# Keys and queries loaded head by head, in transfers of 64 rows with two 2 KB pieces, and an earlier copy of the logits

## The chip, the core and the metric

The kernel runs on one core of a Trainium2 chip. The time of a run is the device time of that core in microseconds. The kernel before was timed three times: 556.40, 557.94 and 558.14 us, median 557.94 us. One more execution, the profiled one, took 561.26 us, and its trace spans 559.5 us from the first to the last instruction. All durations below come from that execution.

## The reference: what is computed

A sparse attention feeds a soft mixture of experts.

```python
# q, k, v: 8 batches x 8 heads x 576 positions x 64
scores = q @ k.T / 8
# heads 0..3: a query sees the 32 keys up to itself (local)
# heads 4..7: a query sees earlier keys at the same position modulo 32 (strided)
attn = softmax(where(mask, scores, -1e9));  x = attn @ v      # x: 4608 x 512

logits = x @ phi                                   # 32 slots, 4 for each of 8 experts
slot_input = softmax(logits, over tokens).T @ x    # 32 x 512
slot_out[e] = relu(slot_input[e] @ w1[e]) @ w2[e]  # w1: 512 x 1024, w2: 1024 x 512
out = softmax(logits, over slots) @ slot_out       # 4608 x 512
```

Everything is in float32. q, k and v hold 9.4 MB each, w1 and w2 16.8 MB each.

## The kernel before

One loop runs over the eight batches. A pass of it has two halves: L deals with the four local heads (x = 0), S with the four strided heads (x = 1). For each half the keys and queries come as rows of 2 KB: eight consecutive positions of one head are one row of 512 numbers, so a head is 72 rows. Eight of those rows (AR) go to the tile `rest`, the other 64 to the tiles `ld`. One `ld` tile holds four heads: partitions are 2 heads (j) times 64 rows, and the free dimension has two pairs of heads (a). `load_kq(b, x)` (lines 158 to 166) issues eight transfers for one half: for keys and for queries, and for each pair a, one of 256 KB into `ld` (line 165) and one of 32 KB into `rest` (line 166). All of them are issued by SP, in program order, together with the values (`load_v1`, line 171; `load_vs`, lines 177 to 181) and the expert weights (`load_weights`, lines 228 and 234, 512 KB each).

PE, ACT and DVE run in the order in which the code is written (a manual schedule); SP and POOL follow their own program order. Every instruction waits only for the data or the buffer that it needs.

`Tl(b)` and `Ts(b)` turn the rows over: `emit_T` makes 8 PE transposes (line 256) for queries, then 8 for keys, `emit_Tr` 8 small ones for `rest` (line 284), and ACT and DVE copy the results from PSUM to `ql`, `kbl`, `qal` (L half: lines 272, 275, 294, 295) and `qs`, `kbs`, `qas` (S half: lines 260, 264, 290, 298). The copies into one tile follow each other, so ACT and DVE alternate there. In the first L half of all, `Tl(0)` stands ahead of the loop; later `Tl(b + 1)` stands in pass b, after the transposes of the local probabilities (`emit_PT(b, 0)`, line 388) and the exponentials of the strided scores (`emit_exp(1)`, line 370).

A pass goes: local scores `emit_Sl` (`sl`), output transposes of the batch before (`emit_X`, `x`), the maximum, `emit_PT(b-1, 1)` and `emit_PTa` (`pt`, `pta`, lines 388 and 396, copied by ACT at 391 and 397), `Ts(b)`, the strided output of the batch before (`emit_AVs`, `as`; `emit_AVa`, `aa`), strided scores `emit_Ss` (`ss`), the slots' logits of the batch before (`emit_LG`, `lg`), their exponentials (`emit_soft`, line 491 on ACT), `emit_PT(b, 0)`, `emit_exp(1)`, `Tl(b+1)`, the copy of the logits from PSUM into `lall` (`st["keep"]`, defined in `emit_soft`, line 498, ACT), the transpose of the slots' exponentials (`emit_dT`, line 502 on PE, line 503 on DVE), the slot inputs (`emit_SI`, `si`) and the local output (`emit_AVl`, `al`). `emit_dT` writes into the same PSUM tile `lg` that the copy of line 498 reads, so it waits for that copy.

Loads are issued far ahead: the keys and queries of an L half right after the transposes of the L half before have read the `ld` tiles, those of an S half likewise. After the loop come the experts (`h`, `so`) and the output (`o`), which draw on 64 weight transfers.

Of the kernel before, what the change touches and what calls it, by code (L numbers as in the profile page):

```python
# [26 lines left out]
PN, TN = 72, 8  # L27
RW = 2 * PN
AUX = 64
AR = AUX // TN  # L30
# [37 lines left out]
def tile_sparse_attention_soft_moe(  # L68
# [12 lines left out]
    nc = tc.nc  # L81
# [28 lines left out]
    def pair2(nm):  # L110
        return psum.tile([P, 2, 512], F32, tag="pp", name=nm, bufs=3)
# [19 lines left out]
    ld = [[fix.tile([P, 2, 512], F32, tag=f"ld{x}{i}", name=f"ld{x}{i}") for i in range(2)] for x in range(2)]  # L131
    rest = fix.tile([P, 2, 512], F32, name="rest")
# [26 lines left out]
    def load_kq(b, x):  # L159
        h0 = 4 * x  # L160
        for i, src in enumerate((k, q)):
            r0 = 32 * x + 16 * i
            for a in range(2):
                rows = src[b, h0 + 2 * a:h0 + 2 * a + 2].rearrange("j (p n) d -> j p (n d)", n=TN)
                nc.sync.dma_start(out=ld[x][i][:, a], in_=rows[:, AR:PN])  # L165
                nc.sync.dma_start(out=rest[r0:r0 + 16, a], in_=rows[:, 0:AR])  # L166

    def load_v1(b):

        for a in range(2):  # L170
            nc.sync.dma_start(out=v1[64 * a:64 * a + 64, a],
                              in_=v[b, 2 * a:2 * a + 2].rearrange("j (s r) d -> r j s d", r=64))
# [63 lines left out]
    def weights_to(n):  # L236
        load_weights(n - len(wts))
# [3 lines left out]
    def two(t, n):  # L241
        return t[:, :, 0:n].rearrange("p a x -> p (a x)") if n == 512 else t[:, :, 0:n]
# [57 lines left out]
    def emit_Sl(b):  # L300
        ps = pair2(f"sl{b}")
        for j in range(2):
            mm(ps[:, j, :], idb, mask_l.unsqueeze(1).to_broadcast([P, 8, 64]), True, False)
        for j in range(2):
            for r in range(4):
                for c in range(4):
                    p0 = PN * j + AR + 4 * (4 * r + c)
                    mm(ps[32 * c:32 * c + 32, j, 128 * r:128 * r + 128], ql[:, j, 4 * r + c],
                       kbl[:, :, :, p0 - 4:p0 + 4].rearrange("p a n r -> p a r n"), False)
        u["sl"] = ps  # L310
# [48 lines left out]
    def emit_max(x):  # L359
        ps = u[("sl", "ss")[x]]  # L360
        _, mx = stats("mx", x)
        for s, m in zip(groups(ps, x), mx):
            nc.vector.tensor_reduce(out=m, in_=s, op=ALU.max, axis=AX.X)  # L363
        for s, o, m in zip(groups(ps, x), probs(x), mx):
            nc.vector.tensor_tensor(out=o, in0=s, in1=bc(m, s.shape[3]), op=ALU.subtract)
# [6 lines left out]
    def emit_sum(x):  # L372
        t, rz = stats("rz", x)
        for s, z in zip(probs(x), rz):
            nc.vector.tensor_reduce(out=z, in_=s, op=ALU.add, axis=AX.X)
        m = 20 if x else 16
        nc.vector.tensor_scalar_add(t[:, 0:m], t[:, 0:m], EPS)
        nc.vector.reciprocal(t[:, 0:m], t[:, 0:m])
        if x == 0:
            u["rz"] = rz[0]  # L380
            return
        for s, z in zip(probs(x), rz):
            nc.vector.tensor_tensor(out=s, in0=s, in1=bc(z, s.shape[3]), op=ALU.mult)

    def emit_PT(b, x, cp):
        ps = pair2(f"pt{b}{x}")
        for g in range(8):
            nc.tensor.transpose(out=ps[:, g // 4, 128 * (g % 4):128 * (g % 4) + 128],  # L388
                                in_=(pl[:, 2 * g:2 * g + 2].rearrange("p a k -> p (a k)") if x == 0 else
                                     psd[:, g].rearrange("p a k -> p (a k)")), identity=ident)  # L390
        cp(out=two(pt, 512), in_=two(ps, 512))  # L391

    def emit_PTa(b, cp):
        ps = small(f"pta{b}")
        for x in range(2):
            nc.tensor.transpose(out=ps[:, 128 * x:128 * x + 128], in_=psd[:, 8 + x].rearrange("p a k -> p (a k)"), identity=ident)
        cp(out=pta, in_=ps[:, 0:256])
# [16 lines left out]
    def emit_AVs(b, cps):  # L414

        ps = pair2(f"as{b}")
        for e in range(2):
            for w in range(2):
                for c in range(4):
                    for j in range(2):  # L420
                        for a in range(2):
                            d = slice(64 * a, 64 * a + NI)
                            o = 128 * (2 * e + w) + 32 * c
                            mm(ps[64 * j:64 * j + 64, a, o:o + 32], vs[d, j, 8 * w + 2 * c + e], pt[d, j, o:o + 32])
        for a in range(2):
            xv = xt[:, a, :].rearrange("p (c e h g) -> p c e h g", c=16, e=2, h=2)
            pv = ps[:, a].rearrange("p (e g c h) -> p c e h g", e=2, g=8, h=2)
            for e in range(2):
                cps[2 * a + e](out=xv[:, :, e], in_=pv[:, :, e])  # L429
# [19 lines left out]
    def emit_X(b, cp):  # L449
        ps = pair2(f"x{b}")  # L450
        for a in range(2):
            for r in range(4):
                nc.tensor.transpose(out=ps[:, a, 128 * r:128 * r + 128], in_=xn[:, r, 128 * a:128 * a + 128], identity=ident)  # L453
        cp(out=two(xt, 512), in_=two(ps, 512))  # L454
# [9 lines left out]
    st = {"m": None}  # L464

    def emit_LG(b, x):

        if x == 0:
            u["lg"] = psum.tile([P, 512], F32, tag="lg", name=f"lg{b}")
        for a in range(2):  # L470
            for t in range(4):
                mm(u["lg"][32 * t:32 * t + 32, 0:128], phs[:, 2 * x + a, :], xt[:, a, 128 * t:128 * t + 128],
                   x == 0 and a == 0, x == 1 and a == 1)
# [6 lines left out]
    def emit_soft(b, n, d):  # L480

        pv = u["lg"][:, 0:128 * n]
        bm = state.tile([P, 1], F32, tag="bm", name=f"bm{b}")
        nc.vector.tensor_reduce(out=bm, in_=pv, op=ALU.max, axis=AX.X)
        ngm = state.tile([P, 1], F32, tag="ngm", name=f"ngm{b}")
        if st["m"] is None:
            nc.vector.tensor_scalar_mul(ngm, bm, -1.0)
        else:
            nc.vector.scalar_tensor_tensor(out=ngm, in0=bm, scalar=-1.0, in1=st["m"], op0=ALU.mult, op1=ALU.min)
        zs = state.tile([P, 1], F32, tag="zs", name=f"zs{b}")  # L490
        nc.scalar.activation(out=d, in_=pv, func=AF.Exp, bias=ngm, accum_out=zs)
        al = None
        if st["m"] is not None:
            al = state.tile([P, 1], F32, tag="al", name=f"al{b}")
            nc.scalar.activation(out=al, in_=st["m"], func=AF.Exp, bias=ngm, scale=-1.0)
        st["m"], st["zs"] = ngm, zs
        u["d"], u["al"] = d, al
        st["keep"] = lambda: nc.scalar.copy(out=lall[:, b:b + n, :].rearrange("p v t -> p (v t)"), in_=pv)  # L498
# [25 lines left out]
    nc.scalar.activation(out=wac, in_=wac, func=AF.Exp)  # L524
    load_kq(0, 0)
    load_kq(0, 1)
    load_v1(0)
    load_vs(0)
# [11 lines left out]
    def Ts(b):  # L540
        emit_T(b, 1, 1, [ACT])
        emit_exp(0)
        emit_T(b, 1, 0, [ACT, DVE])
        emit_Tr(b, 1, [ACT, DVE, ACT, DVE, ACT])
# [3 lines left out]
    for b in range(B):  # L548

        emit_Sl(b)  # L550
        if b > 0:
            emit_X(b - 1, ACT)
        emit_max(0)
        if b > 0:
            emit_PT(b - 1, 1, ACT)
            emit_PTa(b - 1, ACT)
            load_v1(b)
        Ts(b)
        weights_to(2 * b + 2)
        if b < B - 1:  # L560
            load_kq(b + 1, 1)
        emit_sum(0)
        if b > 0:
            emit_LG(b - 1, 0)
            emit_AVs(b - 1, [DVE, ACT, DVE, ACT])
            emit_AVa(b - 1, [ACT, ACT, ACT])
            load_vs(b)
        if b == B - 1:
            weights_to(NWBUF + 5)

        make_v2()
        emit_Ss(b)
        emit_max(1)
        if b > 0:
            emit_LG(b - 1, 1)
            emit_XB(b - 1, ACT)
            emit_soft(b - 1, 1, dd[:, 0])
        emit_PT(b, 0, ACT)
        emit_exp(1)
        if b < B - 1:  # L580
            weights_to(3 * b + 3)
            Tl(b + 1)
        if b < B - 2:
            load_kq(b + 2, 0)
        elif b == B - 2:
            weights_to(NWBUF + 2)
        else:
            weights_to(NWBUF + 11)
        if b > 0:
            st["keep"]()  # L590
            emit_dT(b - 1, 1, u["lg"][:, 128:256], dd[:, 1])
            emit_SI(b - 1)
        emit_AVl(b)
        emit_sum(1)
    weights_to(NWBUF + 12)

    b = B - 1
# [321 lines left out]
```

## Time and profile before

| | before |
|---|---|
| median of 3 runs | 557.94 us |
| profiled execution | 561.26 us (span 559.5 us) |
| PE busy (matmuls) | 312.9 us, 56% of the span |
| DVE busy | 176.0 us, 31% |
| ACT busy | 136.4 us, 24% |
| POOL busy | 43.0 us, 8% |
| bytes moved | 73.31 MB, mean 131 GB/s |
| TensorE clock granted, mean | 0.696 of full speed |

How to read it: the shares are means over two quite different stretches. Up to some 447 us the loop over the batches runs, with 49 to 175 GB/s in the slices of the page; from there to the end the transfers move 213 to 382 GB/s. No engine is busy for more than 56% of the span, so what bounds the kernel is told by who waits for whom, not by the shares. A released wait is named by what came last; an idle time that stands in brackets in a row is the time the engine stood still just before that row.

### The profile page before, as it was taken

The page shows a single profiled execution, that of the slowest core. Times are in us where ns is not written, and L with a number is a line of the kernel's source. Part 1 is how long each engine was busy: PE and PEld are TensorE (multiplying, and loading weights), DVE is VectorE, ACT ScalarE, POOL GpSimd, SP SyncE. Part 2 cuts the span into 40 slices and gives each one's busy share as a digit, 9 for nine tenths or more (in the row PEclk, how much of TensorE's full clock was granted, in tenths as well). Part 3 has the DMA queues.
Part 4 walks back from the last instruction along what each step waited for, and adds up shares of the span by engine and source line. Part 5 has one row for each costly group of instructions (what it writes and reads, how often), then busy time and mean ns, then how long its engine had stood idle before and what let it go on. Part 6 is the DMA issues. An engine that isn't in the chain of part 4 may idle for free.

```text
span 559.5 us, 10346 instructions
## 1 busy us (share of the span) xinstructions
PE 312.9 (56%) x4477; PEld 226.7 (41%) x4477; DVE 176.0 (31%) x369; ACT 136.4 (24%) x297; POOL 43.0 (8%) x43
## 2 busy tenths in 40 slices
PE   3153328443856376636572657165705697779990
PEld 1043225332545245523461445044503474643660
DVE  1030306041522043305230424034402423336781
ACT  1022103232133114311330233021402132211471
POOL 5001100002000200011000200020002003001000
PEclk7565758695767567757675677558956856789996
DMA  2114131223141215121513142313321398699999
GB/s 56 51 52 111 58 116 52 84 71 95 59 150 52 80 64 174 56 80 52 175 67 81 51 136 105 85 49 101 139 84 49 91 292 298 213 310 325 382 368 325
DMA packets 66156, 73.31 MB, mean 131 GB/s; under 512 B 25664, under 2 KB 51648, under 8 KB 66112
## 3 DMA queue, kind: packets, MB, share of 16 engines
q1 hardware_dynamic: 65152, 72.36, 39.7%
q8 instruction: 35, 0.57, 0.4%
q10 hardware_dynamic: 960, 0.30, 0.3%
q14 instruction: 9, 0.07, 0.0%
HBM read 63.22 MB, written 9.44 MB: 130 GB/s over the span
## 4 chain that ended last, share of the span: by engine, by line
DMA 43%; PE 27%; SPq 23%; DVE 2%; issue 2%; ACT 1%; DVEq 0%
DMA ld<-in_q_dram 41%; SPq L166 20%; PE t L256 7%; PE as L246 3%; PE h L737 3%; PE so L835 3%; SPq L165 2%; PE tr L284 2%; PE o L863 2%; DMA ld<-in_k_dram 2%; PE lg L246 2%; PE ss L246 1%; PE si L246 1%; PE aa L246 1%; PE al L246 1%
## 5 line engine op out<-in xcount | busy, mean ns | idle before, releaser
L256 PE MATMUL t<-cf,ld 128*128 128x128 f32 x256 | 59.9, 413 | 182.0 <-DMA ld<-in_q_dram 180.8
L256 PEld LDWEIGHTS t<-cf,ld 128*128 128x128 f32 x256 | 48.4, 216 | 191.5 <-DMA ld<-in_q_dram 105.0
L275 DVE COPY ql<-t 64x512 f32<-64x512 f32 x8 | 5.5, 693 | 148.1 <-ACT ql L275 148.1
L187 POOL COPY v<-v 32x1024 f32<-32x1024 f32 x16 | 16.6, 1035 | 423.8 <-DMA v<-in_v_dram 423.3
L275 ACT COPY ql<-t 64x512 f32<-64x512 f32 x24 | 13.9, 580 | 133.0 <-PE t L256 126.8
L264 DVE COPY kbs<-t 64x1024 f32<-64x1024 f32 x8 | 9.8, 1228 | 90.5 <-ACT kbs L264 90.5
L246 PE MATMUL sl<-kbl,ql 128*32 128x128 f32 x512 | 29.7, 396 | 3.1 <-ACT kbl L294 3.1
L454 ACT COPY xt<-x 128x1024 f32<-128x1024 f32 x8 | 8.1, 1014 | 80.3 <-PE x L453 80.3
L246 PEld LDWEIGHTS al<-v,pt 128*32 128x32 f32 x512 | 22.8, 163 | 10.7 <-issue 9.2
L246 PE MATMUL al<-v,pt 128*32 128x128 f32 x512 | 25.8, 385 | 0.0
L260 ACT COPY qs<-t 128x1024 f32<-128x1024 f32 x8 | 8.1, 1012 | 68.3 <-PE t L256 68.3
L246 PEld LDWEIGHTS sl<-kbl,ql 128*32 128x32 f32 x512 | 18.4, 127 | 15.0 <-ACT kbl L294 4.8
L246 PE MATMUL as<-pt,vs 36*64 36x32 f32 x1024 | 23.1, 256 | 2.2 <-issue 2.2
L246 PEld LDWEIGHTS as<-pt,vs 36*64 36x64 f32 x1024 | 22.0, 178 | 4.8 <-issue 4.4
L502 PE MATMUL lg<-cf,dd 128*128 128x128 f32 x7 | 3.3, 475 | 29.0 <-ACT lall L498 29.0
L246 PE MATMUL ss<-kbs,qs 128*32 128x72 f32 x512 | 15.6, 291 | 3.9 <-issue 2.2
L391 ACT COPY pt<-pt 128x1024 f32<-128x1024 f32 x16 | 16.2, 1010 | 6.2 <-PE pt L388 6.2
L272 DVE COPY kbl<-t 64x512 f32<-64x512 f32 x16 | 11.1, 694 | 19.9 <-ACT kbl L272 19.9
L188 POOL COPY v<-v 32x1024 f32<-32x1024 f32 x16 | 16.6, 1035 | 0.9
L246 PE MATMUL lg<-xt,phs 128*32 128x128 f32 x288 | 15.4, 353 | 1.0 <-ACT xt L429 1.0
L363 DVE TENSOR_REDUCE mx<-ss 128x16 f32<-128x576 f32 (+1 forms) x16 | 8.7, 586 | 22.7 <-PE ss L246 22.7
L284 PEld LDWEIGHTS tr<-cf,rest 32*128 32x128 f32 x128 | 13.7, 199 | 5.3 <-issue 4.6
(192 smaller groups left out, 532.4 us busy)
## 6 DMA issues: line engine op xcount, KB each, us to landing
wb<-in_moe_w_dram SPq DMA_DIRECT2D x41, 512.0 KB
ld<-in_k_dram SPq DMA_DIRECT2D x32, 256.0 KB
ld<-in_q_dram SPq DMA_DIRECT2D x32, 256.0 KB
v<-in_v_dram SPq DMA_DIRECT2D x16, 288.0 KB
vs<-in_v_dram SPq DMA_DIRECT2D x16, 288.0 KB
ld<-in_moe_w_dram SPq DMA_DIRECT2D x4, 512.0 KB
v<-in_moe_w_dram SPq DMA_DIRECT2D x3, 512.0 KB
xt<-in_moe_w_dram SPq DMA_DIRECT2D x3, 512.0 KB
```

Source lines behind the costliest of these rows:

```text
L165: nc.sync.dma_start(out=ld[x][i][:, a], in_=rows[:, AR:PN])
L166: nc.sync.dma_start(out=rest[r0:r0 + 16, a], in_=rows[:, 0:AR])
L187: nc.gpsimd.tensor_copy(out=v2[r + 32:r + 64, a], in_=v1[r:r + 32, a, :, 1:9])
L188: nc.gpsimd.tensor_copy(out=v2[r:r + 32, a], in_=v1[r + 32:r + 64, a, :, 0:8])
L246: nc.tensor.matmul(out=out, lhsT=lhsT, rhs=rhs, start=start, stop=stop, skip_group_check=True)
L256: nc.tensor.transpose(out=tp[:, a, P * n:P * n + P], in_=src[:, a, P * n:P * n + P], identity=ident)
L275: cps[2 * a + e](out=ql[d, :, :, 16 * e:16 * e + 16].rearrange("p j t (r n) -> p (j t) r n", n=4), in_=tp[r, a].rearrange("p (n t r) -> p ...
L284: nc.tensor.transpose(out=tp[:, :, a, :, n, :], in_=rest[32 * x:32 * x + 32, a, P * n:P * n + P], identity=ident[32 * x:32 * x + 32, 32 * ...
L391: cp(out=two(pt, 512), in_=two(ps, 512))
L737: nc.tensor.matmul(out=ph[x][32 * e:32 * e + 32, :], lhsT=sit[:, c, 32 * (4 * g + e):32 * (4 * g + e) + 32], rhs=wts[16 * g + 4 * c + e][: ...
L835: nc.tensor.matmul(out=pos[x][32 * e:32 * e + 32, 0:256], lhsT=hts[g][:, c, 32 * e:32 * e + 32], rhs=wt[:, 256 * e:256 * e + 256], start=( ...
L863: nc.tensor.matmul(out=pq[:, 256 * y:256 * y + 256], lhsT=cts[vb][:, 128 * (2 * (t % 2) + t // 2):128 * (2 * (t % 2) + t // 2) + 128], rhs ...
```

## The change

Two edits. In `load_kq` each transfer now takes one head j of both pairs (64 rows, each with two pieces of 2 KB, one for each pair) in place of both heads of one pair (2 times 64 rows of one piece). The number of transfers, their bytes, their pieces of 2 KB and the places where the data lands are the same. In the loop, `st["keep"]()` moves from behind `Tl(b+1)` to right behind `emit_soft`.

```diff
         for i, src in enumerate((k, q)):
             r0 = 32 * x + 16 * i
-            for a in range(2):
-                rows = src[b, h0 + 2 * a:h0 + 2 * a + 2].rearrange("j (p n) d -> j p (n d)", n=TN)
-                nc.sync.dma_start(out=ld[x][i][:, a], in_=rows[:, AR:PN])
-                nc.sync.dma_start(out=rest[r0:r0 + 16, a], in_=rows[:, 0:AR])
+            rows = src[b, h0:h0 + 4].rearrange("(a j) (p n) d -> j p a (n d)", j=2, n=TN)
+            for j in range(2):
+                nc.sync.dma_start(out=ld[x][i][64 * j:64 * j + 64], in_=rows[j, AR:PN])
+                nc.sync.dma_start(out=rest[r0 + AR * j:r0 + AR * j + AR], in_=rows[j, 0:AR])
...
             emit_soft(b - 1, 1, dd[:, 0])
+            st["keep"]()
         emit_PT(b, 0, ACT)
         emit_exp(1)
...
         if b > 0:
-            st["keep"]()
             emit_dT(b - 1, 1, u["lg"][:, 128:256], dd[:, 1])
```

On SP, the queue that issues the loads, the piece at the end of the first batch's loads reads as follows in the kernel before (`ld_107` is the S half's query tile, `v_115`, `vs` and `val` hold values; behind each name stands the shape of what is written, rows first).

```order
L165 DMA ld_107<-in_q_dram 128x1x512
L166 DMA rest<-in_q_dram 16x1x512
L171 DMA v_115<-in_v_dram 64x18x64 x2
L177 DMA vs<-in_v_dram 36x2x1024
L179 DMA val<-in_v_dram 64x2x64
```

On the same queue, at the same place, the changed kernel has these.

```order
L165 DMA ld_107<-in_q_dram 64x2x512
L166 DMA rest<-in_q_dram 8x2x512
L171 DMA v_115<-in_v_dram 64x18x64 x2
L177 DMA vs<-in_v_dram 36x2x1024
L179 DMA val<-in_v_dram 64x2x64
```

Nothing moved in the queue; lines 165 and 166 have another shape. On the source side the list of pieces of line 165 was 2 heads of 64 rows each and is now 64 rows of 2 heads each; the transfers of the values already had 64 (or 36) rows as the first step of both lists.

On ACT, in the second pass (b = 1), behind the slots' exponentials (line 491), this is the difference (`lall` is the copy of the logits, `ql` and `kbl` are the copies of `Tl(2)`).

```order
 L491 ACTIVATE dd,zs_760<-lg_586,ngm_758 128x128
-L391 COPY pt<-pt_762 128x1024
-L370 ACTIVATE psd<-psd 128x16x36
-L370 ACTIVATE psd<-psd 128x256
-L275 COPY ql<-t_776 64x32x16 x3
-L272 COPY kbl<-t_789 64x4x2x64 x2
-L294 COPY kbl<-tr_802 64x2x4x8 x4
 L498 COPY lall<-lg_586 128x128
+L391 COPY pt<-pt_763 128x1024
+L370 ACTIVATE psd<-psd 128x16x36
+L370 ACTIVATE psd<-psd 128x256
+L275 COPY ql<-t_777 64x32x16 x3
+L272 COPY kbl<-t_790 64x4x2x64 x2
```

The copy of line 498 now stands ahead of the copy of the transposed probabilities, of the exponentials and of the copies that wait for the loads. The orders on PE, DVE and POOL are the same as before.

## Rows read from the trace of the kernel before

**Rows 1.** The page: shares of the chain that ended last, by engine and line.

```profile
DMA 43%; PE 27%; SPq 23%; DVE 2%; issue 2%; ACT 1%; DVEq 0%
DMA ld<-in_q_dram 41%; SPq L166 20%; PE t L256 7%; PE as L246 3%; PE h L737 3%; PE so L835 3%; SPq L165 2%; PE tr L284 2%; PE o L863 2%; DMA ld<-in_k_dram 2%; PE lg L246 2%; PE ss L246 1%; PE si L246 1%; PE aa L246 1%; PE al L246 1%
```

**Rows 2.** Waits, whole span: who waited for whom, us, times, longest.

```profile
PE t L256 <- DMA ld<-in_q_dram: 180.8, 28, 16.4
ACT ql L275 <- PE t L256: 126.8, 8, 25.4
ACT qs L260 <- PE t L256: 68.3, 8, 17.8
```

**Rows 3.** Windows: length, busy of PE to POOL, clock, DMA share, GB/s.

```profile
290.00:296.00 6.00, 0.00 (x0) 0.00 (x0) 0.14 (x1) 2.54 (x7) 0.00 (x0) 0.85 0.13 51
298.00:299.00 1.00, 0.00 (x0) 0.00 (x0) 0.00 (x0) 0.00 (x0) 0.00 (x0) 0.50 1.07 231
336.00:337.00 1.00, 1.00 (x59) 0.80 (x52) 0.52 (x1) 0.56 (x2) 0.00 (x0) 1.00 1.06 389
341.00:345.00 4.00, 4.00 (x96) 3.15 (x92) 0.83 (x2) 1.15 (x5) 0.00 (x0) 0.50 0.15 55
480.00:485.00 5.00, 4.50 (x173) 3.57 (x171) 0.42 (x1) 1.66 (x3) 0.00 (x0) 0.80 0.03 9
```

**Rows 4.** Timeline of SP: start, duration, transfer issued.

```profile
296.25 6.54 SPq L171 DMA_DIRECT2D v<-in_v_dram  x2
306.41 0.76 SPq L166 DMA_DIRECT2D rest<-in_k_dram  x1
312.00 4.99 SPq L166 DMA_DIRECT2D rest<-in_q_dram  x1
```

**Rows 5.** Timeline, an L half: start, duration, engine, instruction, [idle before it].

```profile
288.90 1.04 PE L388 MATMUL pt<-cf,pl 128*128 128x128 f32 x8
291.61 0.99 ACT L370 ACTIVATE psd<-psd 128x576 f32<-128x576 f32 x2
305.91 2.82 PE L256 MATMUL t<-cf,ld 128*128 128x128 f32 x12 [4.92 <-DMA ld<-in_q_dram]
307.06 0.58 ACT L275 COPY ql<-t 64x512 f32<-64x512 f32 x1 [14.46 <-PE t L256]
313.74 0.27 ACT L498 COPY lall<-lg 128x128 f32<-128x128 f32 x1
313.75 0.23 DVE L295 COPY qal<-tr 64x64 f32<-64x64 f32 x1 [0.27 <-ACT kbl L294]
314.06 0.47 PE L502 MATMUL lg<-cf,dd 128*128 128x128 f32 x1 [4.34 <-ACT lall L498]
314.57 0.29 DVE L503 COPY dd<-lg 128x128 f32<-128x128 f32 x1 [0.59 <-PE lg L502]
```

**Rows 6.** Timeline, the S half after it.

```profile
326.37 0.39 ACT L397 COPY pta<-pta 128x256 f32<-128x256 f32 x1
326.55 0.63 PE L256 MATMUL t<-cf,ld 128*128 128x128 f32 x4 [0.98 <-ACT pt L391]
333.59 1.01 ACT L260 COPY qs<-t 128x1024 f32<-128x1024 f32 x1 [6.82 <-PE t L256]
```

**Rows 7.** Timeline, the first batch.

```profile
28.57 0.58 ACT L275 COPY ql<-t 64x512 f32<-64x512 f32 x1 [25.45 <-PE t L256]
35.27 3.74 PE L246 MATMUL sl<-kbl,ql 128*32 128x128 f32 x64 [3.08 <-ACT kbl L294]
53.06 1.01 ACT L260 COPY qs<-t 128x1024 f32<-128x1024 f32 x1 [17.84 <-PE t L256]
```

**Rows 8.** Timeline of PE: two strided outputs, and a gap that no engine releases.

```profile
279.24 3.64 PE L246 MATMUL as<-pt,vs 36*64 36x32 f32 x128
336.38 2.06 PE L246 MATMUL as<-pt,vs 36*64 36x32 f32 x127
340.64 0.31 PE L246 MATMUL as<-pt,vs 36*64 36x32 f32 x1 [2.20 <-issue]
```

## The prediction

> **What bounds the kernel now.** I read the chain that ended last first. Transfers hold 43% of it and SP's issuing 23%, together 66% or 369 us, nearly all in the query loads and in line 166, which issues the `rest` transfers [rows 1]. Then the list of waits: PE stood 180.8 us for loads of `ld`, and behind PE stood ACT, 126.8 us before its first copy of an L half and 68.3 us before its first copy of an S half, 8 times each [rows 2]. So nearly every half ends in a wait for its keys and queries, although they are asked for a whole pass ahead.
>
> The windows tell why they are late. In 290 to 296 us only key and query loads run, and they hold 0.13 of the 16 DMA engines, which is two of the 16, at 51 GB/s; in 298 to 299 us, when a value transfer lands (SP issued it from 296.25 us on), the share is 1.07 at 231 GB/s; with weights it is 1.06 at 389 GB/s [rows 3, 4]. The value transfers begin with a list of 64 rows, the key and query loads with a list of two heads. SP then stands 4.99 us in line 166, and 256 KB at 51 GB/s are 5.1 us: it waits for room behind the transfers before [rows 4]. A half moves 1.18 MB, so 23 us of every half are taken by two engines.
>
> The Trainium skill's page "DMA: Bandwidth & Descriptors", section "Why a DMA increments its semaphore by 16 and not by 1", says that a transfer from SP is spread over the largest number of engines up to 16 that divides the slowest dimension on both sides. By it the old shape gets 2 and the new one 16 (8 for `rest`), and the 0.13 agrees with the 2.
>
> **The change part by part.** The sum is made against the profiled execution, 561.26 us (span 559.5, some 1.8 around it), which is 3.3 us above the median shown.
>
> *The loads.* Number, bytes and pieces stay; the first list becomes 64 rows, as in the value transfers. No row shows this very shape, so I bound its rate by 231 GB/s (the 64-row value transfer with 256 B pieces) and 389 GB/s (weights in 4 KB pieces) above, and 51 GB/s below, where nothing is won. I take 231, the row whose row count is the same. A pass then needs 2.36 MB of keys and queries and 1.18 MB of values at 231, 15.3 us, and three weights of 0.52 MB at 389, 4.0 us: 19 us. SP needs at most 16 issues at 0.76, the two value transfers at 6.54 and a dozen more at 0.76, some 28 us [rows 3, 4]. Both are below the 34 us that I find for a pass below, and each set is asked for about one pass ahead. So the wait goes whole, and what is late next decides the gain.
>
> *L halves, passes 1 to 7.* PE ends the local probabilities' transposes at 289.94. With the rows there, it goes on to 8 query transposes at 0.158 us (0.63 for 4), done by 291.2. ACT, though, has its exponentials until 292.60 and starts its copies then instead of at 307.06: its idle 14.46 goes whole, and ACT is late next, not PE [rows 5, 6]. Over the seven: 126.8 less the first batch's 25.4 is 101.4 us.
>
> *S halves, passes 1 to 7.* ACT is free at 326.76 and PE starts its transposes at 326.55 either way. Eight take 1.27, some 0.2 pass until ACT starts, so `qs` starts at about 328.0 instead of 333.59, and 1.2 of the idle 6.82 stay [rows 6]. Over the seven: 68.3 less 17.8 is 50.5, less 7 x 1.2: 42.1 us.
>
> *First batch.* SP's first eight issues and 1.18 MB at 231 GB/s (5.1 us) put the queries at about 8 us, 8 transposes at 0.235 (2.82 for 12) and the step to ACT make 10.1 for the first copy instead of 28.57: 18.5 us. In its S half PE is free when `sl` ends at 39.01; 8 transposes at 0.235 and 0.2 give 41.1 instead of 53.06: 12.0 us [rows 5, 7]. Ends: 3 us more or less on the first.
>
> The Trainium skill's page "SBUF — State Buffer", section "Door 1: The DMA port swizzle", says that bandwidth follows from how many of the 16 ports the partitions reach, and 64 partitions in a row reach half of them, half of some 436 GB/s. It speaks against halves of 64 rows; 231 is near that half. By it the sum keeps its value, since 231 is what I reckon with; at the weights' rate the first batch would gain 2 us more.
>
> *The copy of the logits.* It costs ACT 0.27 either way. Today PE's transpose at 314.06 waits for it, and DVE's copy follows at 314.57. Moved, the transpose runs during ACT's copies, and DVE's copy follows its own last `qal` copy, at 313.98: 0.6 won, less the 0.27 by which ACT's chain of copies now starts later, 0.3 a pass, 2 us in seven [rows 5]. Of PE's 4.34 us of idle before that transpose only this comes back, since the copies ahead of it must end anyway.
>
> *The clock.* TensorE is granted 0.50 (1.2 GHz) in stretches after PE stood for loads, as in 341 to 345, and 1.00 (2.4 GHz) in 336 to 337, where PE had been at work for some us; the strided output takes 3.64 us at the low level and 2.06 at the high one [rows 3, 8]. Without the loads' wait PE runs from the L half's scores through the S half almost without a pause. That is worth nothing at the least (ACT and DVE copies bind) and at most what an S half costs PE more at the low clock: 1.6 from this row and, I estimate, 1.1 from the strided scores and the transposes behind it, 2.7. Against it stands the 2.20 us gap that PE shows in 340.64 without any releaser [rows 8]; loads hide such gaps now. I take 1.5 a pass, 10.5 us.
>
> *Tail.* Behind the last S half nothing waits for keys or queries. Its weights are asked for by buffers that come free; with the share at 0.03 in 480 to 485 us they have room, so I cost it at nothing [rows 3]. If that cover is gone, some 5 us.
>
> Sum: 101.4 + 42.1 + 30.5 + 2 + 10.5 = 186.5, so 561.3 becomes 374.8; less the 3.3 by which the profiled execution stands above the median, 371.5, said as 371. A pass, now 56.1 us (333.59 less 53.06, over the five passes between [rows 6, 7]), loses 22.3 of it (the terms over seven) and goes to 34.
>
> **The rivals.**
> 1. *Other work comes in the loads' place for more than I allow*: the low clock stays, since PE still stands for the copies of each L half, as it did 4.34 us before line 502 [rows 5], and a gap like that of 2.20 us opens twice a pass. For it: the gap stands in a stretch of high clock, which there will be more of. Against: most passes show no gap like it. 371 + 10.5 + 14 x 2.2 = 412 at the worst, 385 to 412.
> 2. *More speed*: the clock is high throughout, also in the slot inputs and the local output, 1.5 us more a pass, and the S halves give their full 2.7: 371 - 10.5 - 8.4 = 352, 345 to 356. Against: in each L half PE still waits for the copies.
> 3. *The change doesn't do what it says*: the new shape too runs on two engines at 51 GB/s. The waits stay and the copy's 2 us are hidden behind them: 558. For it: the destination is still 128 rows in all and the pieces are as before. Against: the 1.07 of the 64-row transfers. The skill's page "DMA: Bandwidth & Descriptors" has a rule of the like outcome in "Rules for kernel authors": two transfers to disjoint halves of the partitions gain nothing, one of 128 is to be used. By that rule the time would stay at 558; the trace bears it out poorly, since the 128-row transfer here holds but 0.13.
> 4. *Slower*: the transfer of one head goes to one engine, as a transfer of two heads now goes to two. Then 51 GB/s become 25.5 and the 369 us of the chain double: 927. It decides below 51 GB/s. Against: the value transfers take two heads too and hold all engines.
>
> **How the numbers follow.** Chances: forecast 0.71 (its own range 357 to 385: the clock's term between 0 and 19, the start's 3, the tail's 5), rival 1 0.12, rival 2 0.11, rival 3 0.04, rival 4 0.02. The range of 8 in 10 leaves out the far ends of rivals 1 and 2 and all of 3 and 4: 350 to 397. A change under 0.3% can't be told from none here. Faster are the forecast, rivals 1 and 2: 0.94. Within 0.3% is rival 3, 0.04; slower rival 4, 0.02.
>
> **What would show it.** The DMA share near 1 while `ld` loads run, and line 166 at 0.8 us instead of 5; no row of PE waiting for `ld` except in the first batch; ACT's idle before L275 near nothing and before L260 near 1.2; TensorE at 1.00 in the strided output of most passes; the transpose of line 502 ahead of ACT's last copies; a pass of 33 to 36 us. Wrong it would be if line 166 still stood for us, if PE waited for values, or if the weights were late behind the last pass.

## The result, and the profile after

The changed kernel takes 354.18 us (median of 4, 350.55 to 358.08) against 557.17 us before in the same comparison: a ratio of 0.6306 [0.6272, 0.6341]. Two further comparisons gave 356.24 us, 0.6379 [0.6352, 0.6406], and 355.72 us, 0.6318 [0.6279, 0.6357]. The times are medians of all executions and the ratios those of the fast ones alone, since some executions of one and the same kernel run 1% or 2% longer at a lower granted clock. The forecast was 371 us; the time lies inside the range of 350 to 397 and 3 us below the likeliest case's own range, 357 to 385. The profiled execution took 350.55 us, which is the fastest of them; its span is 348.8 us and its mean granted clock 0.869, where before it was 0.696.

The page of the changed kernel: the chain by engine, and PE's group of strided outputs (busy us, mean ns).

```profile
PE 52%; ACT 21%; DVE 17%; issue 4%; DMA 3%; DVEq 0%; SPq 0%; ACTq 0%
L246 PE MATMUL as<-pt,vs 36*64 36x32 f32 x1024 | 16.5, 220 | 0.0
```

DMA and SP's issuing, two thirds of the chain before [rows 1], are 3% now. What is left is PE, ACT and DVE handing work to each other. The waits over the whole span, who for whom, us, times and longest:

```profile
PE si L246 <- DVE dd L503: 44.3, 7, 7.4
ACT ql L275 <- PE t L256: 9.3, 1, 9.3
ACT qs L260 <- PE t L256: 4.9, 1, 4.9
PE t L256 <- DMA ld<-in_q_dram: 4.7, 1, 4.7
```

Against [rows 2], PE's wait for loads went from 180.8 us to 4.7, and ACT's two waits behind PE from 126.8 and 68.3 us to 9.3 and 4.9; all that is left of the three stands in the first batch. At the head of PE's list stands another now: PE before the slot inputs (`si`), 44.3 us in seven. Most of it was there before, ahead of line 502: 29.0 us in seven, 4.34 of them in [rows 5]. The timeline of an L half shows it (start, duration, engine, instruction, idle before it and what ended that):

```profile
158.87 1.04 PE L388 MATMUL pt<-cf,pl 128*128 128x128 f32 x8
159.74 1.91 PE L256 MATMUL t<-cf,ld 128*128 128x128 f32 x16
161.57 1.01 ACT L370 ACTIVATE psd<-psd 128x576 f32<-128x576 f32 x2
162.19 0.33 PE L502 MATMUL lg<-cf,dd 128*128 128x128 f32 x1
162.46 0.58 ACT L275 COPY ql<-t 64x512 f32<-64x512 f32 x1
165.95 0.48 SPq L166 DMA_DIRECT2D rest<-in_q_dram  x1
169.14 0.23 DVE L295 COPY qal<-tr 64x64 f32<-64x64 f32 x1 [0.27 <-ACT kbl L294]
169.40 0.29 DVE L503 COPY dd<-lg 128x128 f32<-128x128 f32 x1
169.84 1.93 PE L246 MATMUL si<-xn,dd 128*32 128x512 f32 x8 [7.32 <-DVE dd L503]
171.52 3.67 PE L246 MATMUL al<-v,pt 128*32 128x128 f32 x64
```

Beside [rows 5], the 16 transposes follow the local probabilities at once; ACT's first copy (L275) has no idle time before it where it had 14.46 us; line 166 takes 0.48 us where it took 4.99 [rows 4]. The transpose of line 502 now runs ahead of ACT's copies. DVE's copy of it (L503) still waits in DVE's order behind the last `qal`, and PE stands 7.32 us for it. Next, the S half:

```profile
181.64 1.02 ACT L391 COPY pt<-pt 128x1024 f32<-128x1024 f32 x1
181.79 2.01 PE L256 MATMUL t<-cf,ld 128*128 128x128 f32 x16
182.54 0.39 ACT L397 COPY pta<-pta 128x256 f32<-128x256 f32 x1
182.92 1.02 ACT L260 COPY qs<-t 128x1024 f32<-128x1024 f32 x1
```

The first copy, L260, follows `pta` (the copy of L397) with no idle time; before, 6.82 us stood there [rows 6]. And PE begins its transposes at 181.79, inside ACT's copy of `pt`, which in [rows 6] was named as what released them.

Windows of the changed kernel (length, busy of PE, PEld, DVE, ACT and POOL, granted clock, DMA share, GB/s): loads of keys and queries while PE stands, PE's work right behind that, and weights.

```profile
165.70:167.70 2.00, 0.00 (x0) 0.00 (x0) 1.32 (x3) 0.78 (x2) 0.00 (x0) 0.50 1.06 201
170.00:173.00 3.00, 3.00 (x36) 1.75 (x35) 0.75 (x1) 0.00 (x0) 0.00 (x0) 0.50 0.67 165
265.00:270.00 5.00, 3.04 (x18) 2.85 (x18) 3.10 (x7) 1.01 (x1) 0.43 (x1) 0.79 1.06 389
```

The loads hold all 16 engines (1.06, before 0.13) and move 201 GB/s, four times the 51 of [rows 3]. After PE's standing the clock is 0.50, that is 1.2 GHz, while `si` and `al` run.

The first copies of ACT:

```profile
12.43 0.58 ACT L275 COPY ql<-t 64x512 f32<-64x512 f32 x1 [9.31 <-PE t L256]
23.94 1.01 ACT L260 COPY qs<-t 128x1024 f32<-128x1024 f32 x1 [4.86 <-PE t L256]
```

They stood at 28.57 and 53.06 [rows 7]. The passes from the second to the seventh, from one such L260 to the next, last 33.3 us in the mean (32.4 to 33.8) in place of 56.7.

Last, PE and DVE in the last pass, where no keys or queries are left to load. Before:

```profile
452.04 3.64 PE L246 MATMUL as<-pt,vs 36*64 36x32 f32 x128
463.02 1.97 PE L461 MATMUL xb<-cf,xt 128*128 128x128 f32 x8
468.58 0.48 PE L502 MATMUL lg<-cf,dd 128*128 128x128 f32 x1 [2.70 <-ACT lall L498]
469.44 1.94 PE L246 MATMUL si<-xn,dd 128*32 128x512 f32 x8 [0.38 <-DVE dd L503]
471.15 3.64 PE L246 MATMUL al<-v,pt 128*32 128x128 f32 x64
474.88 1.29 DVE L409 TENSOR_TENSOR xn<-al,rz 128x512 f32<-128x512 f32 x2 [2.69 <-PE al L246]
```

After:

```profile
250.94 2.07 PE L246 MATMUL as<-pt,vs 36*64 36x32 f32 x128
257.77 1.09 PE L461 MATMUL xb<-cf,xt 128*128 128x128 f32 x8
260.66 0.33 PE L502 MATMUL lg<-cf,dd 128*128 128x128 f32 x1 [0.93 <-ACT lall L498]
261.38 1.07 PE L246 MATMUL si<-xn,dd 128*32 128x512 f32 x8 [0.38 <-DVE dd L503]
262.26 1.93 PE L246 MATMUL al<-v,pt 128*32 128x128 f32 x64
264.28 1.29 DVE L409 TENSOR_TENSOR xn<-al,rz 128x512 f32<-128x512 f32 x2 [1.02 <-PE al L246]
```

The last L260 starts at 448.44 before and at 248.96 after. From there to L409 it is 26.44 us before and 15.32 after, with a mean granted clock of 0.56 before and 1.00 after: most rows of PE take little more than half the time. This stretch became 11.1 us shorter without having any load of keys or queries to wait for.

### The profile page after: what moved, and what is told of

Its sections match the earlier page's. It is cut to its first block, busy times and chain, and to the rows that moved or that the text cites. A ratio compares the mean times of both kernels' runs of the same rounds, so it can differ in the third digit from the quotient of the medians.

```text
span 348.8 us, 10348 instructions
## 1 busy us (share of the span) xinstructions
PE 259.0 (74%) x4477; PEld 187.0 (54%) x4477; DVE 175.3 (50%) x369; ACT 134.8 (39%) x297; POOL 43.5 (12%) x43
## 4 chain that ended last, share of the span: by engine, by line
PE 52%; ACT 21%; DVE 17%; issue 4%; DMA 3%; DVEq 0%; SPq 0%; ACTq 0%
PE sl L246 9%; PE al L246 5%; PE h L737 4%; PE so L835 4%; PE si L246 4%; PE ss L246 4%; ACT ql L275 4%; DVE kbl L272 3%; PE as L246 3%; PE t L256 3%; ACT pt L391 3%; ACT kbl L272 3%; PE o L863 3%; PE x L453 2%; PE lg L246 2%
## 5 line engine op out<-in xcount | busy, mean ns | idle before, releaser
L246 PE MATMUL si<-xn,dd 128*32 128x512 f32 x56 | 12.7, 992 | 44.3 <-DVE dd L503 44.3
L256 PE MATMUL t<-cf,ld 128*128 128x128 f32 x256 | 33.4, 285 | 5.3 <-DMA ld<-in_q_dram 4.7
L256 PEld LDWEIGHTS t<-cf,ld 128*128 128x128 f32 x256 | 29.3, 146 | 8.9 <-issue 5.6
L246 PE MATMUL al<-v,pt 128*32 128x128 f32 x512 | 22.6, 348 | 0.0
L272 DVE COPY kbl<-t 64x512 f32<-64x512 f32 x16 | 11.1, 694 | 19.9 <-ACT kbl L272 19.9
L275 DVE COPY ql<-t 64x512 f32<-64x512 f32 x8 | 5.5, 693 | 30.5 <-ACT ql L275 30.5
L275 ACT COPY ql<-t 64x512 f32<-64x512 f32 x24 | 13.9, 577 | 15.5 <-PE t L256 9.3
L246 PE MATMUL ss<-kbs,qs 128*32 128x72 f32 x512 | 12.4, 243 | 7.5 <-issue 4.2
L409 DVE TENSOR_TENSOR xn<-al,rz 128x512 f32<-128x512 f32 x16 | 10.3, 686 | 14.0 <-PE al L246 14.0
L246 PEld LDWEIGHTS as<-pt,vs 36*64 36x64 f32 x1024 | 15.7, 135 | 1.8 <-issue 1.4
L246 PE MATMUL as<-pt,vs 36*64 36x32 f32 x1024 | 16.5, 220 | 0.0
L246 PE MATMUL lg<-xt,phs 128*32 128x128 f32 x288 | 13.7, 307 | 2.3 <-ACT xt L429 2.2
L246 PEld LDWEIGHTS ss<-kbs,qs 128*32 128x32 f32 x512 | 10.1, 117 | 9.7 <-issue 6.1
```

The source lines that it names most:

```text
L246: nc.tensor.matmul(out=out, lhsT=lhsT, rhs=rhs, start=start, stop=stop, skip_group_check=True)
L256: nc.tensor.transpose(out=tp[:, a, P * n:P * n + P], in_=src[:, a, P * n:P * n + P], identity=ident)
L272: cps[2 * a + e](out=kbl[d, a, e::2].rearrange("p n (j r) -> p n j r", j=2)[:, :, :, AR:PN], in_=tp[r, a].rearrange("p (n j r) -> p n j r" ...
L275: cps[2 * a + e](out=ql[d, :, :, 16 * e:16 * e + 16].rearrange("p j t (r n) -> p (j t) r n", n=4), in_=tp[r, a].rearrange("p (n t r) -> p ...
L409: nc.vector.tensor_tensor(out=xn[:, :, 0:256].rearrange("p r (a j d) -> p j r a d", a=2, j=2)[:, j], in0=ps[:, j].rearrange("p (r a d) -> ...
```

## The experiments

**Which of the two edits.** One kernel takes the loads alone, with the copy of the logits at its old place; it ran twice, the second time beside the changed kernel. Against the changed kernel:

```diff
             emit_soft(b - 1, 1, dd[:, 0])
-            st["keep"]()
...
         if b > 0:
+            st["keep"]()
             emit_dT(b - 1, 1, u["lg"][:, 128:256], dd[:, 1])
```

> The loads in the new shape, the copy of the logits at its old place behind Tl(b+1). Theory (PE's transpose of line 502 then waits for ACT's copies again, which sets DVE's copy back by 0.6 us in six passes and by about 2 us in the last, less 0.27 us a pass of ACT's chain): about 4 us more than the changed kernel, 354 to 356 us where the changed one takes 350 to 352. Rival (PE's whole wait for that copy, 4.3 us a pass today, is on the path once the loads no longer hide it): 25 us more, about 377. Rival (the copy's place is hidden): the same as the changed kernel.

> The loads in the new shape, the copy at its old place, beside the whole change on the same chip. Theory (the copy is worth some 0.3 us in each of six passes and 2 us in the last): 3 to 5 us more than the next run. Rival (its place is worth nothing): no difference. Rival (more than the theory has, because PE's slot inputs start later at a low clock): 6 us or more.

> The whole change, for the comparison with the run ahead of it: 352 to 357 us.

Measured: 358.3 us, 0.6423 [0.6403, 0.6444], and the second time 360.41 us, 0.6397 [0.6353, 0.6441], with the changed kernel beside it at 0.6318 [0.6279, 0.6357]. The loads alone carry all but some 4 us: (0.6397 - 0.6318) x 558 = 4.4. The two intervals just touch, so the size is rough. The theory (about 4 us) fits and 25 us is out; between it and the rivals of nothing and of 6 us or more the times alone decide poorly. Where the 4 us lie is seen in the trace of the loads alone:

```profile
172.23 0.27 ACT L498 COPY lall<-lg 128x128 f32<-128x128 f32 x1
172.24 0.23 DVE L295 COPY qal<-tr 64x64 f32<-64x64 f32 x1 [0.27 <-ACT kbl L294]
172.55 0.48 PE L502 MATMUL lg<-cf,dd 128*128 128x128 f32 x1 [7.02 <-ACT lall L498]
173.06 0.29 DVE L503 COPY dd<-lg 128x128 f32<-128x128 f32 x1 [0.60 <-PE lg L502]
```

From the start of the last `qal` copy to that of L503 it is 0.82 us here and 0.26 in the changed kernel, 0.56 a pass, 3.4 in the six passes that have both copies; the last pass, without `qal`, adds 1.8 (PE's wait before L502 is 2.71 here and 0.93 in the changed kernel). Less the 0.27 by which ACT's copies start later (1.6 in six) that is 3.5.

The other edit alone is the kernel before with `st["keep"]()` moved.

> The copy of the logits moved, the loads in the old shape. Theory (the half ends in the wait for the loads, whatever stands ahead of it): 557 us as before, within 0.5%, with PE's wait before line 502 gone and its wait for the loads longer by as much. Rival (the copy is on the path already): 3 to 5 us less.

Measured: 556.83 us, 0.9978 [0.9956, 1.0]. Its waits:

```profile
PE t L256 <- DMA ld<-in_q_dram: 177.4, 28, 15.3
```

The time is the same, as the theory had it, but not quite for its reason. PE's wait before line 502 went from 29.0 us to 1.2, yet the wait for loads did not become longer (180.8 before): PE now stands 27.1 us before `si`, for DVE's copy L503, where it had stood 2.7. The half ends as before, and the copy's place is hidden.

**What sets the rate of a load.** Each transfer of the changed kernel is cut into two, first n rows and then the other 64 - n, with n = 48, 57, 62 and 61:

```diff
-                nc.sync.dma_start(out=ld[x][i][64 * j:64 * j + 64], in_=rows[j, AR:PN])
+                for lo, hi in ((0, n), (n, 64)):
+                    nc.sync.dma_start(out=ld[x][i][64 * j + lo:64 * j + hi], in_=rows[j, AR + lo:AR + hi])
```

> Each transfer of 64 rows into ld becomes two, of 48 and of 16 rows: same pieces, twice the number of ld transfers. Theory (what counts is into how many engines up to 16 the count of rows divides: 16 for both): the same as the changed kernel within 2%, since SP has the time for 16 more issues a pass. Rival (number and size of transfers count): slower by 10 us or more. It is the control for the next three, which have the same number of transfers.

> As before it, 57 and 7 rows. Theory (57 divides into 3 engines, 7 into 7): 0.93 MB of a half at three times 25.5 GB/s take 12.2 us, 24.4 a pass, with values and weights some 33, about the length of a pass of 33.8: 354 to 375 us. Rival (only a first list shorter than 16 confines a transfer, 57 rows spread like 64): the same as 48 and 16.

> As before it, 62 and 2 rows. Theory (62 divides into 2 engines): 1.02 MB of a half at 51 GB/s, 19.9 us where the kernel before had 23.1: 525 to 545 us, the DMA share at 0.13 again. Rival (a list of 62 rows spreads like one of 64, or the two pieces a row are what helped): 350 to 360.

> As before it, 61 and 3 rows. Theory (61 is prime: one engine): 1.00 MB of a half at 25.5 GB/s, 39 us, a pass of some 92 us, 800 to 860 us in all, share 0.06. Rival (a long list spreads): 350 to 360.

Measured: 357.69 us with 48 (0.6427 [0.6377, 0.6477]), 417.83 with 57 (0.7499 [0.7459, 0.754]), 548.02 with 62 and 829.28 with 61 (one execution each, so no interval). Bytes, pieces and the number of transfers are the same in all four. Windows inside the loads, 57 rows first, then 62, then 61:

```profile
205.00:220.00 15.00, 6.36 (x33) 4.84 (x37) 3.38 (x9) 4.57 (x11) 4.14 (x4) 0.60 0.33 93
```

```profile
295.00:310.00 15.00, 9.11 (x99) 7.01 (x99) 4.39 (x11) 3.71 (x9) 4.14 (x4) 0.66 0.15 51
```

```profile
370.00:390.00 20.00, 0.00 (x0) 0.00 (x0) 0.00 (x0) 0.00 (x0) 0.00 (x0) 0.53 0.08 29
```

With 62 rows the rate is the 51 GB/s of before, with 61 it is 29, a little over half of that. The window of 57 holds values and short parts too; where the share falls to 0.19, in 205 to 206 us, the rate is 76 GB/s. PE's wait for `ld` comes back, in all 45.7 us with 57, 170.1 with 62 and, the row of it, with 61:

```profile
PE t L257 <- DMA ld<-in_q_dram: 461.6, 16, 38.3
```

48 and 64 are multiples of 16; the largest divisors up to 16 of 57, 62 and 61 are 3 (of 3 x 19), 2 and 1. The Trainium skill's page "DMA: Bandwidth & Descriptors", section "Why a DMA increments its semaphore by 16 and not by 1", names that divisor as the number of engines; these three kernels agree, with 76, 51 and 29 GB/s where three, two and one engine at 25.5 GB/s each, half of the 51 of two, would give 76.5, 51 and 25.5. That fewer rows on fewer engines, and not the cut itself, cost the time is told by 48, where the same cut costs 0.8% to 1.9% over the changed kernel, by the three ratios. The times with 62 and 61 came out about as expected (548 against 525 to 545, 829 within 800 to 860). For 57 the expectation was too low, 354 to 375 against 418. The rate fits the mechanism: the long part of a pass's loads is 24.4 us at three engines, by 1.87 MB and 76.5 GB/s. But the pass lasts 39.8 us; the other 15.4, values and the short parts among them, I had reckoned at 9, and they were not taken apart.

**Who holds PE before the slot inputs.** The transpose of the slots' exponentials (L502) and its copy (L503) move up between the queries' and the keys' transposes and copies, and `si` goes to a PSUM tile of another kind, so that it can start ahead of the last copies:

```diff
-        ps = small(f"si{b}")
+        ps = pair2(f"si{b}")[:, 0, :]
...
-    def Tl(b):
+    def Tl(b, done=0):
         emit_T(b, 0, 1, [ACT, DVE, ACT, ACT])
+        if done:
+            emit_dT(done - 1, 1, u["lg"][:, 128:256], dd[:, 1])
...
-            Tl(b + 1)
+            Tl(b + 1, b)
...
-        if b > 0:
+        if b == B - 1:
             emit_dT(b - 1, 1, u["lg"][:, 128:256], dd[:, 1])
+        if b > 0:
             emit_SI(b - 1)
```

> The changed kernel, with emit_dT written behind the first transposes of Tl(b+1), emit_SI in a PSUM buffer of its own kind (pair2 in place of the single small one), so that the slot inputs and the local output run on PE while ACT and DVE copy. Theory (what bounds a pass of the changed kernel is ACT's and DVE's copies into ql and kbl, 6.9 us, and behind them in a row DVE's dd, PE's slot inputs and local output at the low clock, and the local scores): slot inputs and local output leave the path, 5 to 6 us a pass in six passes, about 320 us. Rival (DVE's work behind the copies, acc, xn, the sums and the normalisation, 4.6 us, takes their place): 340 us or more.

Measured: 322.52 us, 0.5784 [0.5755, 0.5812], mean clock 0.913. That is near the 320 expected, and about 9% faster than the changed kernel (322.52 / 354.18). In its trace L503, `si` and the local output run, or start, while ACT and DVE still copy:

```profile
152.30 0.29 DVE L503 COPY dd<-lg 128x128 f32<-128x128 f32 x1
152.74 1.06 PE L246 MATMUL si<-xn,dd 128*32 128x512 f32 x8 [1.58 <-DVE zs L505]
153.60 3.60 PE L246 MATMUL al<-v,pt 128*32 128x128 f32 x64
157.65 0.23 DVE L295 COPY qal<-tr 64x64 f32<-64x64 f32 x1 [0.27 <-ACT kbl L294]
```

PE's 7.32 us before `si` are 1.58. So what bounded the changed kernel's L halves was the copies into `ql`, `kbl` and `qal` and, behind them one after the other, `si`, `al` and `sl`. A pass is 28.8 us in the mean. The local scores `sl` still come behind the last copy.

**What the low clock costs.** The changed kernel with 26 products of constants, read by nobody, on PE in its idle time before `si`, in passes 1 to 6:

```diff
             emit_dT(b - 1, 1, u["lg"][:, 128:256], dd[:, 1])
+            if b < B - 1:
+                junk = pair2(f"junk{b}")
+                for _ in range(26):
+                    mm(junk[:, 0, :], idb, idb.unsqueeze(1).to_broadcast([P, 4, 128]))
```

> The changed kernel with 26 matmuls of 512 columns without use (bf16, into a PSUM buffer that nobody reads) on PE between line 502 and the slot inputs of passes 1 to 6, where PE idles 7.3 us for DVE's copy. Nothing of the result changes. Theory (the clock falls to 1.2 GHz in that idle time, and the slot inputs, 1.93 us against 1.07 in the last pass, and the local output, 2.2 to 3.4 against 1.9, pay for it on the path): 1.5 to 2.3 us a pass, 9 to 14 us less than the changed kernel, with the clock at 1.00 in the slot inputs. Rival (their length is set by the weight loads or by DVE, not by the clock): no less, or more where the junk overruns the idle time.

Measured: 348.2 us, 0.6233 [0.621, 0.6257], mean clock 0.924.

```profile
158.77 5.78 PE L246 MATMUL junk<-cb 128*128 128x512 bf16 x26
166.30 1.07 PE L246 MATMUL si<-xn,dd 128*32 128x512 f32 x8 [1.76 <-DVE dd L503]
167.16 1.96 PE L246 MATMUL al<-v,pt 128*32 128x128 f32 x64
```

`si` takes 1.07 us in place of 1.93 and `al` 1.96 in place of 3.67, 2.6 in this pass; as `al` takes 2.5 to 3.7 us in the six passes of the changed kernel, it is 2.0 in the mean. The three ratios of the changed kernel less this one give 4 to 8 us in place of the 9 to 14 expected, so part of what PE wins here is given back. The traces show where: the seven stretches from ACT's first copy L275 to its first copy L260 are 12.4 us shorter in sum than in the changed kernel, as expected, but those from L260 to the next L275 are 6.6 us longer (3 to 4 against the two other traces of the changed kernel). In the latter lie idle times of PE that nothing releases, as the 2.20 us of [rows 8]. They add up to 12.4 us here, in these two groups, and to 6.1 in the changed kernel:

```profile
PE aa L246 <- issue: 8.7, 5, 2.5
PE ss L246 <- issue: 3.7, 3, 1.9
```

What opens them is not shown.

**The longer passes of the faster version.** Its trace shows DVE's softmax held up where POOL copies values:

```profile
132.22 1.03 POOL L187 COPY v<-v 32x1024 f32<-32x1024 f32 x1 [21.63 <-DMA v<-in_v_dram]
132.24 1.05 DVE L377 TENSOR_SCALAR rz<-rz 128x20 f32<-128x20 f32 x1
133.63 2.49 DVE L383 TENSOR_TENSOR psd<-psd,rz 128x576 f32<-128x576 f32 x2
```

In the next kernel two transfers bring those values, and POOL copies nothing there:

```diff
+            for j in range(2):
+                nc.sync.dma_start(out=v2[64 * a:64 * a + 64, a, j],
+                                  in_=v[b, 2 * a + j, 32:544].rearrange("(s r) d -> r s d", r=64))
...
-            nc.gpsimd.tensor_copy(out=v2[r + 32:r + 64, a], in_=v1[r:r + 32, a, :, 1:9])
-            nc.gpsimd.tensor_copy(out=v2[r:r + 32, a], in_=v1[r + 32:r + 64, a, :, 0:8])
```

> The version with slot inputs and local output under the copies, with the shifted values v2 loaded from memory (two transfers of 128 KB more for each pair of heads) in place of POOL's four copies a pass. In that version some passes take 30 us and others 27, and in a long one DVE's small sum takes 1.05 us instead of 0.17 and its normalisation 2.49 instead of 1.09 while POOL copies. Theory (DVE is held up by POOL's copies where they meet): all passes at about 27.5, 6 to 9 us less, 313 to 317 us. Rival (the long passes come from elsewhere, and 0.5 MB more a pass at some 200 GB/s crowds the loads): 322 us or more.

Measured: 322.83 us, 0.5789 [0.5767, 0.5812], no different from 0.5784. The hold-up is gone from the trace:

```profile
129.93 0.18 DVE L379 TENSOR_SCALAR rz<-rz 128x20 f32<-128x20 f32 x1
130.46 1.09 DVE L385 TENSOR_TENSOR psd<-psd,rz 128x576 f32<-128x576 f32 x2
```

But the time is as it was, as the rival had it. Passes of 28 to 30 us are still there among those of 27. In this trace they are the three in which PE stands still for 1.5 to 1.9 us behind the strided output with no releaser (28.6, 28.9 and 30.1 us; 0.9 or less in the three of 27.0 to 27.1); the part from L275 to L260 is 13.7 us in all of them. What opens these gaps is not shown, nor whether the added loads play a part in them.

The changed kernel was also run once more beside this one:

> The changed kernel once more, beside the next one and with more runs, so that the small differences to it (the copy's place, the matmuls without use) can be told: 350 to 355 us, a ratio to the kernel before of 0.628 to 0.636.

It gave 356.24 us and 0.6379, told above, a little over both expectations.

## Why the prediction came out as it did

The forecast of 371 us was 17 us too high, with the time inside its range. The profiled executions differ by 561.26 - 350.55 = 210.7 us; the sum was 186.5. Term by term, in us:

| term | predicted | measured | from |
|---|---|---|---|
| first copy of ACT | 18.5 | 16.1 | 28.57 to 12.43 |
| first S half | 12.0 | 13.0 | 24.49 to 11.51 between the two first copies |
| L halves, wait | 101.4 | 101.4 | no idle before L275 in all seven |
| S halves, wait | 42.1 | 50.5 | no idle before L260 in all seven |
| copy of the logits | 2 | 4.4 | the two runs side by side |
| clock and gaps | 10.5 | 25.3 | what is left |

*The loads: right.* The mechanism and the 101.4 us came out as worked: the wait goes whole and ACT's exponentials are late next. The transfers were not 231 but 201 GB/s, with no effect past the first batch. The Trainium skill's page "SBUF — State Buffer", section "Door 1: The DMA port swizzle", has 64 partitions in a row reach half the ports; the 201 GB/s beside the weights' 389, both at a share of 1.06, agree. The weights also come in longer pieces (4 KB against 2 KB), and no run here tells the two apart.

*The S halves: a misread row.* I left 1.2 us of idle in each, since the transposes of [rows 6] had "ACT pt" as the releaser of their 0.98 us. In the changed kernel PE starts them during that copy, and in three other S halves of the kernel before it had done so too (at 211.69 us, where the copy runs from 211.53 on). So that copy had not released them; what changed is when their rows come. PE's first eight transposes are then done before ACT is free, and the whole 50.5 us went.

*The first batch: 2.3 us late.* I had the queries at about 8 us; ACT's copy came at 12.43 and not at 10.1, and PE's wait for `ld` there is still 4.7 us. The error lies within the 3 us that I gave it.

*The copy: right place, too small.* The 0.3 a pass holds (0.56 less 0.27), in six passes. I forgot that the last pass has no `qal`; it wins 1.8. By the rows that makes 3.5 us, by the two runs 4.4.

*The clock: the term that was mis-sized.* "I take 1.5 a pass, 10.5 us", with 19 as the far end, came out at 25.3. I had priced the strided output from rows at both levels (3.64 and 2.06), estimated the scores and the transposes behind it, and taken about half of that for each of seven passes. The last pass shows best what was left out. There `si` goes from 1.94 to 1.07, `al` from 3.64 to 1.93, `xb` from 1.97 to 1.09, beside `as`. The kernel with the loads alone, its copy where it was before, takes 17.1 us for the same stretch (L260 at 255.47, L409 at 272.58). So of the 11.1 us the copy's place won 1.8 and the loads, with the clock, 9.3, where I had 1.5.

Over the seven S halves with loads it is 15.3 us beyond the idle times (116.7 gained between the first copies, 101.4 of it idle), 2.2 each. Over the L halves it is 3.2 (53.7 less 50.5), which the copy's six times 0.56 cover: there the clock won next to nothing. The page's `as` is 16.5 us in all eight passes, 2.06 a pass, where before it was 23.1, four of the eight at 3.64. That the clock, and not the loads, is the cause in the last pass rests on PE's rows above; that keeping PE at work raises it is shown by the 26 products, where `si` and `al` ran at half the time.

The size of the term differs from execution to execution, and 25.3 is taken between a slow one of the kernel before and the fastest of the changed one. With the two other traces of the changed kernel (355.86 and 356.95 us) the same sum leaves 19.8 and 18.6, and between the medians 17.6; it is above 10.5 each time. The last pass is a case of it. With the copy alone and the loads as before, `as` took 3.64 but `xb`, `si` and `al` 1.09, 1.06 and 1.93: the clock came back within the pass, which took 20.7 us in place of 26.4, with the gain from the copy's place in it. In the second trace of the loads alone `si` and `al` stayed at the low level (1.93 and 3.64), and it took 19.8. The changed kernel has 15.3 in all three traces.

Gaps like that of 2.20 us [rows 8] did not become more in the changed kernel: PE's idle times without a releaser add up to 6.0 us before (2.2, 2.2 and 1.6, by line and operation) and 6.1 after (4.4 and 1.7). So rival 1 fell. Its reason is not refuted: with PE kept at work by the 26 products, and the clock at 0.924, these gaps were twice as long in sum.

*The tail: right.* From that L409 to the last instruction it is 84.6 us before and 84.5 after.

*The rivals.* Rival 2, 345 to 356 us, is nearly what came, by half of its reason: the S halves gave 2.2 of their 2.7 and the last pass 9.3, but `si` and `al` stay at the low level in most passes (3.67 above), since PE still stands 7.3 us for the copies, as I had held against it. Executions lie between 350.6 and 359.8 us; in the two traces that I compared for it, `al` takes 18.7 us in one of 350.55 and 20.9 in one of 355.86, so the pass in which the clock comes back early is part of that spread. Rival 3 fell with the share of 1.06. The Trainium skill's page "DMA: Bandwidth & Descriptors", section "Rules for kernel authors", says of two transfers to disjoint halves that they share the same 16 engines, and advises one transfer to 128 partitions. Here the one 128-row transfer held two engines (0.13), and the halves are faster; the measurement decides. Rival 4 did not come. Where its condition was made, one engine with 61 rows, the time was 829 us against the 927 that doubling the chain gave.

## What to carry to other kernels

A transfer whose outermost list is short (two heads here), or has a count whose largest divisor up to 16 is small (57, 61 and 62 here), moves at a fraction of the rate however many partitions it fills; read the DMA share in a window where that transfer alone runs, and not the mean. Where such a wait goes, the gain is set by who is late next, found in the same rows, and every PE row that stands at the low clock behind the wait is to be priced at the high one, in stretches that have no such wait too, with a range, since the clock comes back at another place from execution to execution. An idle time's named releaser is to be doubted where what follows also reads a late transfer.

## What was not expected of the hardware

Transfers of 57 and 7 rows are slower than those of 48 and 16 by 60 us of this kernel, and 61 and 3 rows take it past the kernel before by 272 us, with the same bytes, pieces and transfers; the second was expected, the first came out much longer. With 26 products keeping PE at work, the idle times of PE that nothing releases went from 6.1 to 12.4 us. While POOL copied values, a DVE operation on 128x20 took 1.05 us in place of 0.18 and one on 128x576 2.49 in place of 1.09; taking the copies away gave those times back and won no time that could be measured.
